# Turned rows with q lo twice for each head: score and state products on 128 rows instead of 64 and a padded state

## Chip, cores and metric

The kernel runs on one core of one Trainium2 chip. The metric is the device time of one execution in microseconds (us); the median of three runs stands for a kernel. Times inside an execution come from one profiled execution.

## What is computed

A gated linear attention over 768 tokens (4 sequences, 8 heads of 48), its rows through a gated product (the first MoE, dense, 1536 wide), and the result through eight experts, each token to the one with the largest logit.

```python
state = f[t][..., None] * state + k[t] outer v[t]     # f = sigmoid(f_logit), per batch and head, 48x48
y[t]  = q[t] @ state
x     = ((y @ w_a) * (y @ w_b)) @ w_out               # 3072 tokens x 384
e     = argmax(x @ w_gate)                            # of 8 experts
out   = gate * sigmoid(x @ w_output_gate)[e] * (relu(x @ w1[e]) @ w2[e])
```

All inputs are float32. The kernel keeps that precision by splitting every operand in a high and a low part (hi, lo) and adding the products that count.

## The kernel before

The 3072 tokens are 24 tiles of 128 (six chunks of each of four sequences); two tiles are one of 12 blocks. For each tile fourteen steps turn q, k, v and f into rows x of the attention; for each block the first MoE runs 12 times (`f` from 0 to 11) over `m_ab` (L816 to L818, 18 products) and `m_out` (L840 to L842, 6 products). Blocks 0 and 1 run while the weights are loaded and decoded: their order comes from a list of nominal times (T0, TAU). From block 2 on, `attend` (L1010) weaves the steps of the two tiles of the next block between the products of the present one, by the table `at`: for the first tile of a block scores at f = 4 and 5, for the second both at f = 6. The order on each engine is set at compile time by a scheduler that goes by program order, by readiness in its own timeline and by free buffers; some instructions are kept in program order by hand (`in_order`, L301). Tiles of one tag share its buffers.

The steps that matter here:

- `a_log` (L601) writes lh and ll, hi and lo of log f, one buffer each; `a_cum` (L633) sums them over the tokens with a triangular matrix (L636 for lh, L637 for ll) into a PSUM bank of tag "at", from which ScalarE makes eq and ek.
- `a_z` (L655) writes q and k, scaled, as float16 into z. Of a pair of heads it holds ten blocks of 64 columns: q hi twice for head 0, q hi twice for head 1, q lo for both heads, then k hi and lo, k lo and hi. On VectorE: L660 (k hi), L664 (q hi, twice), L665 (q lo); on GpSimd from tile 4 on: L661 (k lo). SyncE then issues one transposing DMA (L667) into zT, 20 blocks of 128 rows (four pairs of five). There is one zT buffer.
- `a_u` (L671) splits the state U before the chunk: hi on ScalarE (L683), lo on GpSimd (L684), and a copy of hi into U3, zero-padded to both heads, on GpSimd (L685).
- `a_kv` (L687) sums k times v of the chunk (L698 to L700), and VectorE updates U.
- `a_score` (L716), called twice a tile for four heads each: for each head a product on 128 rows (L726: k hi and lo against q hi twice) and one on 64 rows (L727: k hi against q lo). VectorE masks the result (sm, L729), ScalarE rounds it to Sh (L731), VectorE subtracts for Sl (L732).
- `a_av` (L737, L742 to L744) multiplies Sh and Sl by v; `a_inter` (L746) multiplies q by the state: for each pair two products of 48 columns (L758) and one of 96 columns (L760) of q lo with U3.
- `a_turn` (L766) and `a_x` (L777) turn the rows and split them into xh (ScalarE, L796) and xl (VectorE, L797), the moving operands of `m_ab` for the next block.

In the first blocks `conv_o` (L524) turns each of 12 pieces of w_out through two PSUM banks of tag "at" (L535, L545), the same tag as cumulative sums and scores.

Of the kernel before, what the change touches and what calls it, by code (L numbers as in the profile page):

```python
# [9 lines left out]
F16 = mybir.dt.float16  # L10
# [12 lines left out]
def general_path(nc, tc, q, k, v, f_logit, w_a, w_b, w_out, w_gate, w_ogate, w1, w2, out, cons):  # L23
    """the whole computation again, for values that the fast path doesn't carry"""
# [11 lines left out]
    with ExitStack() as ctx:  # L36
# [9 lines left out]
        # ---- recurrence over the tokens, one by one  # L46
# [52 lines left out]
        # ---- first MoE and the routing, 128 tokens at a time  # L99
        with tc.tile_pool(name="g_m1", bufs=1) as sp:  # L100
# [4 lines left out]
            for nm, w, n, m in (("a", w_a, KD, FF), ("b", w_b, KD, FF), ("o", w_out, NF, DM)):  # L105
                wt[nm] = tl("g_w" + nm, [P, n, m])
                for kk in range(n):
                    for c in range(m // DM):
# [39 lines left out]
                        # below float32's range: zero  # L148
# [98 lines left out]
        # ---- the experts, 128 slots at a time  # L247
# [57 lines left out]
def kernel(  # L305
# [46 lines left out]
    # ---------------------------------------------------------------- pools  # L352
# [17 lines left out]
    # ------------------------------------------------------------ constants  # L370
    # n(t): number of steps of the static slope up to token t of a chunk
# [72 lines left out]
    # routing state: (token, scale) per token, counts, sums of the softmax, ranges  # L444
# [9 lines left out]
    # DRAM scratch: rows of the first MoE by token (and a row of zeros), slot table  # L454
# [6 lines left out]
    # ---------------------------------------------------- weights, hi and lo  # L461
# [16 lines left out]
    def decoded(raw, n, on_pool):  # L478
        """384 columns of a weight as float32, times 2^WS"""
# [7 lines left out]
        # The upper word as a float has the double's exponent over 8. Times 2^(WS - 126) its  # L487
        # three upper exponent bits are clear, as long as the double is below 2^(128 - WS):
        # the sums tell. Below 2^(-112 - WS) it comes to nothing.
# [34 lines left out]
    def conv_o(f, raw, n, on_pool):  # L524
# [7 lines left out]
        # w_out @ [w_gate | w_output_gate] for these rows  # L532
# [18 lines left out]
    # -------------------------------------------------------------- attention  # L551
# [15 lines left out]
    # Heads in pairs, the first of a pair on the lower 64 partitions and the second on the upper:  # L567
    # of a pair, q hi twice for each head, q lo, k hi and lo, k lo and hi
    HP = H // 2
    z_n = [tl(f"z{n}", [P, HP, 10, 64], F16) for n in range(NZ)]  # L570
    U2 = [tl(f"U2{n}", [P, HP, 2, D], F16) for n in range(2)]
    U3 = [tl(f"U3{n}", [P, HP, 2, D], F16) for n in range(2)]
# [4 lines left out]
    for x in U2 + U3 + g_n:  # L577
        nc.gpsimd.memset(x, 0.0)

    def part(o):  # L580
        """the partitions of the pairs' first or second heads"""
        return slice(64 * o, 64 * o + D)
# [18 lines left out]
    def a_log(i):  # L601
        s = st[i]
        f, vin = s["f"], s["v"]
        nc.scalar.activation(out=f, in_=f, func=AF.Exp, scale=-1.0)
        nc.scalar.activation(out=f, in_=f, func=AF.Ln, scale=c_st, bias=c_st)
        s["lh"] = tl("lh", [P, H, D], F16)
        s["ll"] = tl("ll", [P, H, D], F16)
        nc.vector.tensor_copy(out=s["lh"], in_=f)
        fast(i).tensor_tensor(out=s["ll"], in0=f, in1=s["lh"], op=ALU.subtract)

    def squares(i, n, src, scale, junk):
        """the sum of squares of every token's row"""
# [42 lines left out]
    def a_z(i):  # L655
# [3 lines left out]
        kh, kl = z[:, :, 6:10:3, :D], z[:, :, 7:9, :D]  # L659
# [5 lines left out]
        nc.vector.tensor_tensor(out=z[:, :, 4:6, :D], in0=qe, in1=z[:, :, 0:4:2, :D], op=ALU.subtract)  # L665
        s["T"] = tl("zT", [P, 5 * HP, P], F16, 1)
# [4 lines left out]
    def a_u(i):  # L671
        """the state before this chunk, hi and lo"""
# [6 lines left out]
        if c > 0:  # L679
            u2, u3 = s["u2"], s["u3"] = U2[i % 2], U3[i % 2]  # L680
            for o in range(2):
                hi, lo = u2[part(o), :, o], u2[part(1 - o), :, o]
                nc.scalar.activation(out=hi, in_=U[b][part(o)], func=AF.Copy)  # L683
                nc.gpsimd.tensor_tensor(out=lo, in0=U[b][part(o)], in1=hi, op=ALU.subtract)  # L684
                nc.gpsimd.tensor_copy(out=u3[part(o), :, o], in_=hi)  # L685

    def a_kv(i):  # L687
# [6 lines left out]
        for h in range(H):  # L694
            a, o = divmod(h, 2)
            kh, kl = s["z"][:, a, 6 + 3 * o], s["z"][:, a, 7 + o]
# [19 lines left out]
    def a_score(i, u):  # L716
# [6 lines left out]
        for j in range(4):  # L723
            half = slice(64 * u, 64 * u + 64)
            k2, ql = T[:, 5 * j + 3 + u], T[half, 5 * j + 2]
            nc.tensor.matmul(sc[:, j], k2, T[:, 5 * j + u], start=True, stop=False)  # L726
            nc.tensor.matmul(sc[:, j], k2[half], ql, start=False, stop=True)  # L727
# [18 lines left out]
    def a_inter(i):  # L746
# [8 lines left out]
        for a in range(HP):  # L755
            for o in range(2):
                first_of = a == 0 and o == 0
                nc.tensor.matmul(pi[:, 2 * a + o], T[:, 5 * a + o], s["u2"][:, a, o], start=first_of, stop=False)  # L758
            two = pi[:, 2 * a : 2 * a + 2]
            nc.tensor.matmul(two, T[:, 5 * a + 2], s["u3"][:, a], start=False, stop=(a == HP - 1))  # L760
# [5 lines left out]
    def a_turn(i):  # L766
        """rows to columns by DMA, two bytes at a time: the words' lower and upper halves apart"""
# [37 lines left out]
    # -------------------------------------------------------------- first MoE  # L805
# [81 lines left out]
    def r_rank(j):  # L887
        """every token's slot: its expert's base and the tokens before it"""
# [19 lines left out]
    def free_order(key, ins):  # L908
        """scatters of one table go to rows of their own: they don't wait for each other"""
# [50 lines left out]
    # ------------------------------------------------------- experts' weights  # L960
# [3 lines left out]
    def load_expert(e, g, part):  # L964
        """two f-tiles of the e-th expert in line: part 0 of w1, part 1 of w2"""
# [23 lines left out]
    # --------------------------------------------------- program, first phase  # L989
# [10 lines left out]
    def route(j, f):  # L1000
        """the tokens of block j, sent to their experts in steps"""
# [50 lines left out]
    # the first two blocks run while the weights come: emission by nominal time  # L1052
# [41 lines left out]
    # -------------------------------------------------------------- second MoE  # L1094
    # The experts stand in a line: first the one with the most tokens before the last block, then
    # the others by their number of tokens, most first, each place with slots of its own number.
    # No token of the last block goes to the first half of the first place's slots, so these can
    # start before that block ends.
# [14 lines left out]
    def tiles_of(e):  # L1113
        """tiles of the e-th place: first slot and size"""
# [12 lines left out]
    def choose_first():  # L1127
        """the expert with the most tokens before the last block gets the first place"""
# [24 lines left out]
    def first_tokens(n):  # L1153
        """half n of the first place's slots"""
# [17 lines left out]
    def e_turn(e, u):  # L1172
        """rows to columns by DMA, two bytes at a time: the words' lower and upper halves apart"""
# [50 lines left out]
    def e_h(e, f, n=None):  # L1224
        """the first product of the e-th place for f, or of half n of the first place"""
# [4 lines left out]
        # hi, then lo with the tokens of a pair first: both parts of these stand together  # L1230
# [17 lines left out]
    def is_pair(m):  # L1248
        """a tile so small that both parts of h stand beside each other in one product"""
# [56 lines left out]
    def line_up(pc):  # L1306
        """the experts in their line, and whether one has too many tokens for its place"""
# [46 lines left out]
    def check_path():  # L1354
        """anything that the fast path doesn't carry: values out of its range or overfull experts"""
# [36 lines left out]
    def ahead(e, turn, columns, f):  # L1392
        """the input of the e-th place, while the one before is computed"""
# [144 lines left out]
```

## Time and profile before

| | |
|---|---|
| median of 3 runs | 931.11 us (930.51 to 933.27) |
| span of the profiled execution | 931.4 us |
| TensorE busy | 862.8 us, 93% |
| TensorE weight loads busy | 797.7 us, 86% |
| VectorE busy | 549.6 us, 59% |
| ScalarE busy | 448.0 us, 48% |
| GpSimd busy | 360.0 us, 39% |

The profiled execution has its span as its own time; it lies 0.3 us above the median. An instruction's duration on TensorE runs from its start to its modelled end, and products overlap: what a product costs in a dense series is seen from start to start, not from its duration. "Idle before" is the time that the engine stood before a group, with what ended it. The last part of the span, from some 627 us on, has no attention in it: it is the last block and the experts.

### The profile page before, as it was taken

What the parts mean: (1) busy time and instruction counts of PE and PEld (TensorE: products, weight loads), DVE (VectorE), ACT (ScalarE), POOL (GpSimd) and SP (SyncE); (2) the same over time, 40 slices, a digit from 0 to 9 for tenths busy, and PEclk for the clock granted to TensorE, in tenths of its full rate; (3) what the DMA queues carried; (4) which work ended last, traced back from release to release, by engine and by line L of the source; (5) the groups of instructions that cost most, each with busy time, mean ns of one, the idle gap of its engine ahead of it and who ended that gap; (6) DMA issues with size and microseconds to landing.
All of it is one profiled execution on the core that took longest, in us unless ns stands there. A gap on an engine that the chain in (4) does not pass through costs nothing.

```text
span 931.4 us, 18145 instructions
## 1 busy us (share of the span) xinstructions
PE 862.8 (93%) x6733; PEld 797.7 (86%) x6733; DVE 549.6 (59%) x1289; ACT 448.0 (48%) x1104; POOL 360.0 (39%) x428
## 2 busy tenths in 40 slices
PE   2689789989999999999999999999978999999993
PEld 1477789978989898989899999999878999999993
DVE  8887875554746474646555565642546666666630
ACT  6756655533545454536454554432424434445530
POOL 4444664352535353535445363412344231131111
PEclk9997999989999999999999999999989999999997
DMA  9874535462516252443526161211348644665610
GB/s 202 186 167 137 158 89 111 88 69 55 107 38 122 38 116 44 90 71 57 95 43 117 36 124 20 60 33 50 122 120 225 172 125 159 189 175 155 185 58 22
DMA packets 247756, 98.53 MB, mean 106 GB/s; under 512 B 210600, under 2 KB 243717, under 8 KB 247658
## 3 DMA queue, kind: packets, MB, share of 16 engines
q1 hardware_dynamic: 242538, 87.22, 42.3%
q0 software_dynamic: 4320, 10.03, 3.5%
q8 instruction: 55, 0.90, 0.4%
q14 instruction: 43, 0.35, 0.1%
q10 hardware_dynamic: 800, 0.02, 0.1%
HBM read 63.56 MB, written 10.49 MB: 80 GB/s over the span
## 4 chain that ended last, share of the span: by engine, by line
PE 70%; DMA 9%; DVE 8%; issue 7%; ACT 2%; POOL 2%; SPq 0%; POOLq 0%; DVEq 0%; ACTq 0%
PE ps_ab L816 9%; PE ps_ab L817 9%; PE ps_ab L818 9%; PE ps_out L301 5%; PE ps_out L842 4%; PE ps_out L841 4%; PE ps_yk L301 4%; PE ps_out L840 4%; PE ps_ab L1221 3%; PE ps_ab L1220 3%; PE ps_ab L1222 3%; PE ps_at L727 3%; PE ps_at L726 3%; DMA slots<-info,di 2%; DMA zT<-z 2%
## 5 line engine op out<-in xcount | busy, mean ns | idle before, releaser
L816 PE MATMUL ps_ab<-xh,wab 128*128 128x256 f32 x864 | 253.0, 293 | 5.5 <-DVE gf L824 3.8
L817 PE MATMUL ps_ab<-xl,wab 128*128 128x256 f32 x864 | 248.8, 288 | 0.5 <-DVE xl L797 0.5
L818 PE MATMUL ps_ab<-xh,wab 128*128 128x256 f32 x864 | 248.5, 288 | 0.2 <-POOL wab L520 0.2
L828 POOL TENSOR_TENSOR gl<-gf,gh 128x256 fp32r<-128x256 f32 x144 | 111.6, 777 | 244.7 <-ACT gh L827 243.3
L816 PEld LDWEIGHTS ps_ab<-xh,wab 128*128 128x128 f32 x864 | 167.1, 194 | 9.4 <-DVE gf L824 4.7
L817 PEld LDWEIGHTS ps_ab<-xl,wab 128*128 128x128 f32 x864 | 167.1, 193 | 2.3 <-DVE xl L797 1.8
L818 PEld LDWEIGHTS ps_ab<-xh,wab 128*128 128x128 f32 x864 | 167.2, 193 | 0.7 <-POOL wab L520 0.3
L824 DVE SCALAR_TENSOR_TENSOR gf<-ps_ab,asb 128x256 f32<-128x256 f32 x144 | 60.3, 419 | 81.4 <-ACT asb L823 76.0
L827 ACT ACTIVATE gh<-gf 128x256 fp32r<-128x256 f32 x144 | 59.9, 417 | 93.4 <-DVE gf L824 90.0
L841 PE MATMUL ps_out<-wo,gh 128*128 128x400 f32 x264 | 93.0, 352 | 2.2 <-DVE wo L547 2.2
L842 PE MATMUL ps_out<-wo,gl 128*128 128x400 f32 x264 | 92.2, 357 | 2.2 <-POOL gl L828 2.2
L840 PE MATMUL ps_out<-wo,gh 128*128 128x400 f32 x264 | 89.9, 348 | 1.3 <-ACT wo L546 1.3
L1294 POOL DMA_INDIRECT out_dram<-ys,tab x29 | 30.0, 1033 | 145.4 <-ACT ys L1289 139.9
L823 ACT ACTIVATE asb<-ps_ab 128x256 f32<-128x256 f32 x144 | 54.4, 379 | 58.1 <-PE ps_ab L818 57.9
L1221 PE MATMUL ps_ab<-xsl,wab 128*128 128x256 f32 (+5 forms) x216 | 73.5, 341 | 0.1
L1220 PE MATMUL ps_ab<-xsh,wab 128*128 128x256 f32 (+5 forms) x216 | 73.5, 341 | 0.1
L1222 PE MATMUL ps_ab<-xsh,wab 128*128 128x256 f32 (+5 forms) x216 | 73.3, 339 | 0.0
L977 DVE TENSOR_TENSOR wab<-raw,wab 128x768 fp32r<-128x768 f32 x48 | 46.6, 972 | 40.4 <-ACT wab L301 40.0
L1234 ACT ACTIVATE h<-ps_ab 128x256 fp32r<-128x256 f32 (+5 forms) x72 | 34.7, 483 | 69.3 <-PE ps_ab L1222 64.6
L1238 DVE SCALAR_TENSOR_TENSOR h<-ps_ab,h 128x64 fp32r<-128x64 f32 (+5 forms) x96 | 41.1, 450 | 36.7 <-ACT h L1234 36.7
L729 DVE TENSOR_TENSOR sm<-ps_at,mask 128x512 f32<-128x512 f32 x48 | 33.0, 688 | 45.0 <-PE ps_at L727 44.8
L732 DVE TENSOR_TENSOR Sl<-sm,Sh 128x512 f16<-128x512 f32 x48 | 33.9, 706 | 40.0 <-ACT Sh L731 40.0
(261 smaller groups left out, 1977.7 us busy)
## 6 DMA issues: line engine op xcount, KB each, us to landing
raw<-in_moe_w_dram SPq DMA_DIRECT2D x64, 384.0 KB
in_f<-in_f_logit_dram SPq DMA_DIRECT2D x24, 192.0 KB
in_q<-in_q_dram SPq DMA_DIRECT2D x24, 192.0 KB
in_k<-in_k_dram SPq DMA_DIRECT2D x24, 192.0 KB
in_v<-in_v_dram SPq DMA_DIRECT2D x24, 192.0 KB
raw<-in_moe_w_a_dram SPq DMA_DIRECT2D x12, 384.0 KB
raw<-in_moe_w_b_dram SPq DMA_DIRECT2D x12, 384.0 KB
raw<-in_moe_w_out_dram SPq DMA_DIRECT2D x12, 384.0 KB
```

The lines of the kernel that those rows point to most:

```text
L301: return lambda *a, **k: tc.keep_in_program_order(op(*a, **k))
L816: nc.tensor.matmul(pab[:, a], wh[:, kk, o : o + P], xh[:, kk], start=(kk == 0), stop=False)
L817: nc.tensor.matmul(pab[:, a], wh[:, kk, o : o + P], xl[:, kk], start=False, stop=False)
L818: nc.tensor.matmul(pab[:, a], wl[:, kk, o : o + P], xh[:, kk], start=False, stop=(kk == KD - 1))
L824: nc.vector.scalar_tensor_tensor(out=gf, in0=pab[:, 1], scalar=2.0**-WS, in1=asb, op0=ALU.mult, op1=ALU.mult)
L828: nc.gpsimd.tensor_tensor(out=gl, in0=gf, in1=gh.bitcast(F32), op=ALU.subtract)
L840: nc.tensor.matmul(o, gh[:, ts], wh[:, u], start=(f == 0), stop=False)
L841: nc.tensor.matmul(o, gh[:, ts], wl[:, u], start=False, stop=False)
L842: nc.tensor.matmul(o, gl[:, ts], wh[:, u], start=False, stop=(f == NF - 1))
L1220: nc.tensor.matmul(ph, wh[:, kk, o : o + P], sh[:, kk, us], start=(kk == 0), stop=False)
L1221: nc.tensor.matmul(ph, wh[:, kk, o : o + P], sl[:, kk, us], start=False, stop=False)
L1222: nc.tensor.matmul(ph, wl[:, kk, o : o + P], sh[:, kk, us], start=False, stop=(kk == KD - 1))
```

## The change

z has twelve blocks for each pair instead of ten: q hi twice for each head, then q lo twice for each head, then k hi and lo of the first head, k hi and lo of the second. One more copy on VectorE for each tile writes q lo a second time. zT has 24 blocks of 128 rows instead of 20. The second score product of a head takes the same 128-row operand as the first, against q lo twice, so that k lo times q lo is added, which was left out. The state products are two of 48 columns for each head, both on 128 rows with the same u2; U3 and its two copies for each tile go. To make room, lh and ll take the buffers of Sh and Sl (tags "Sh" and "Sl", one buffer each). Comments were removed in other places, so later lines keep their text and shift a little.

```diff
+    NB = 6
     HP = H // 2
-    z_n = [tl(f"z{n}", [P, HP, 10, 64], F16) for n in range(NZ)]
+    z_n = [tl(f"z{n}", [P, HP, 2 * NB, 64], F16) for n in range(NZ)]
-    U3 = [tl(f"U3{n}", [P, HP, 2, D], F16) for n in range(2)]
...
-        s["lh"] = tl("lh", [P, H, D], F16)
-        s["ll"] = tl("ll", [P, H, D], F16)
+        s["lh"] = ab.tile([P, H, D], F16, name="lh", tag="Sh")
+        s["ll"] = ab.tile([P, H, D], F16, name="ll", tag="Sl")
...
-        kh, kl = z[:, :, 6:10:3, :D], z[:, :, 7:9, :D]
+        kh, kl = z[:, :, 8:12:2, :D], z[:, :, 9:12:2, :D]
...
-        nc.vector.tensor_tensor(out=z[:, :, 4:6, :D], in0=qe, in1=z[:, :, 0:4:2, :D], op=ALU.subtract)
-        s["T"] = tl("zT", [P, 5 * HP, P], F16, 1)
+        ql = z[:, :, 4:8:2, :D]
+        nc.vector.tensor_tensor(out=ql, in0=qe, in1=z[:, :, 0:4:2, :D], op=ALU.subtract)
+        nc.vector.tensor_copy(out=z[:, :, 5:8:2, :D], in_=ql)
+        s["T"] = tl("zT", [P, NB * HP, P], F16, 1)
...
-            u2, u3 = s["u2"], s["u3"] = U2[i % 2], U3[i % 2]
+            u2 = s["u2"] = U2[i % 2]
...
-                nc.gpsimd.tensor_copy(out=u3[part(o), :, o], in_=hi)
...
-            kh, kl = s["z"][:, a, 6 + 3 * o], s["z"][:, a, 7 + o]
+            kh, kl = s["z"][:, a, 8 + 2 * o], s["z"][:, a, 9 + 2 * o]
...
-            half = slice(64 * u, 64 * u + 64)
-            k2, ql = T[:, 5 * j + 3 + u], T[half, 5 * j + 2]
-            nc.tensor.matmul(sc[:, j], k2, T[:, 5 * j + u], start=True, stop=False)
-            nc.tensor.matmul(sc[:, j], k2[half], ql, start=False, stop=True)
+            k2 = T[:, NB * j + 4 + u]
+            nc.tensor.matmul(sc[:, j], k2, T[:, NB * j + u], start=True, stop=False)
+            nc.tensor.matmul(sc[:, j], k2, T[:, NB * j + 2 + u], start=False, stop=True)
...
-                first_of = a == 0 and o == 0
-                nc.tensor.matmul(pi[:, 2 * a + o], T[:, 5 * a + o], s["u2"][:, a, o], start=first_of, stop=False)
-            two = pi[:, 2 * a : 2 * a + 2]
-            nc.tensor.matmul(two, T[:, 5 * a + 2], s["u3"][:, a], start=False, stop=(a == HP - 1))
+                u2 = s["u2"][:, a, o]
+                nc.tensor.matmul(pi[:, 2 * a + o], T[:, NB * a + o], u2, start=True, stop=False)
+                nc.tensor.matmul(pi[:, 2 * a + o], T[:, NB * a + 2 + o], u2, start=False, stop=True)
```

## Rows read from the trace of the kernel before

**Rows 1.** The page, busy time of each engine over the span.

```profile
PE 862.8 (93%) x6733; PEld 797.7 (86%) x6733; DVE 549.6 (59%) x1289; ACT 448.0 (48%) x1104; POOL 360.0 (39%) x428
```

**Rows 2.** Busy time by stage: PE, PEld, DVE, ACT, POOL, clock, DMA share, GB/s.

```profile
0.00:140.00 140.00, 100.77 (x746) 83.25 (x747) 117.73 (x247) 88.71 (x246) 71.89 (x88) 0.94 0.65 156
140.00:200.00 60.00, 60.00 (x558) 55.62 (x557) 35.97 (x98) 30.62 (x88) 27.46 (x36) 1.00 0.54 94
...
215.00:627.00 412.00, 411.19 (x3678) 379.00 (x3678) 231.83 (x579) 200.79 (x530) 178.38 (x223) 1.00 0.38 70
```

**Rows 3.** Timeline of TensorE, one score step: start, duration, line, rows*columns, shapes.

```profile
350.84 0.23 PE L726 MATMUL ps_at<-zT 128*128 128x128 f16 x1
351.00 0.23 PE L727 MATMUL ps_at<-zT 64*128 64x128 f16 x1
...
352.12 0.39 PE L816 MATMUL ps_ab<-xh,wab 128*128 128x256 f32 x1
```

**Rows 4.** Timeline of TensorE, dense series on 128 rows, and what follows.

```profile
362.68 0.18 PE L742 MATMUL ps_yk<-vv,Sh 128*128 128x48 f16 x1
...
363.11 0.18 PE L744 MATMUL ps_yk<-vv,Sl 128*128 128x48 f16 x1
363.13 0.22 PE L726 MATMUL ps_at<-zT 128*128 128x128 f16 x1
...
375.01 0.34 PE L636 MATMUL ps_at<-lh,tri 128*128 128x384 f16 x1
375.18 0.19 PE L744 MATMUL ps_yk<-vv,Sl 128*128 128x48 f16 x1
...
375.38 0.18 PE L743 MATMUL ps_yk<-vv,Sh 128*128 128x48 f16 x1
```

**Rows 5.** Groups of TensorE's weight loads by line: count | busy us, mean ns | idle before.

```profile
L726 PEld LDWEIGHTS <-zT 128*128 128x128 f16 x192 | 18.7, 98 | 20.8 <-DMA zT<-z 7.0 <-issue 2.3
```

**Rows 6.** Busy time by stage of line L726 alone: PE, PEld (counts in brackets).

```profile
0.00:140.00 140.00, 8.78 (x32) 3.42 (x32) 0.94 0.65 156
...
215.00:627.00 412.00, 31.02 (x136) 12.91 (x135) 1.00 0.38 70
```

**Rows 7.** Timeline of ScalarE around 203 us: idle before, and what ended it.

```profile
203.32 0.52 ACT L604 ACTIVATE in_f<-in_f 128x384 f32<-128x384 f32 x1 [8.27 <-DMA in_f<-in_f_logit_dram]
```

**Rows 8.** Timeline of TensorE, state products of one tile.

```profile
221.26 0.20 PE L760 MATMUL ps_yk<-U,zT 128*128 128x96 f16 x1
...
221.54 0.20 PE L760 MATMUL ps_yk<-U,zT 128*128 128x96 f16 x1
```

**Rows 9.** Timeline of SyncE's queue, transposes of a block's first and second tile.

```profile
339.59 2.93 SPq L667 DMA_TRANSPOSE zT<-z  x1
...
357.67 3.07 SPq L667 DMA_TRANSPOSE zT<-z  x1
```

**Rows 10.** The chain that ended last, around 407 us: start, length, what.

```profile
406.97 6.04 DMA zT<-z
```

**Rows 11.** Timeline of VectorE, lh for the next pair of tiles.

```profile
337.70 0.35 DVE L608 CAST lh<-in_f 128x384 f16<-128x384 f32 x1
```

**Rows 12.** Timeline of GpSimd, k lo of a block's first tile.

```profile
338.39 1.17 POOL L661 TENSOR_TENSOR z<-ek,z 128x384 f16<-128x384 f32 x1 [1.10 <-DVE z L660]
```

**Rows 13.** Timelines of GpSimd and TensorE: tile 4's ll, and its cumulative product.

```profile
48.90 2.51 POOL L609 TENSOR_TENSOR ll<-in_f,lh 128x384 f16<-128x384 f32 x1 [3.58 <-DVE lh L608]
...
134.21 0.29 PE L545 MATMUL ps_at<-wg,woT 128*128 128x16 f32 x2
134.35 0.32 PE L636 MATMUL ps_at<-lh,tri 128*128 128x384 f16 x1
```

**Rows 14.** Timelines of VectorE and TensorE where a block begins.

```profile
332.16 0.56 DVE L797 TENSOR_TENSOR xl<-xt,xh 128x384 fp32r<-128x384 f32 x1 [0.59 <-ACT xh L796]
333.66 0.34 PE L637 MATMUL ps_at<-ll,tri 128*128 128x384 f16 x1
...
334.36 0.28 PE L816 MATMUL ps_ab<-xh,wab 128*128 128x256 f32 x1
```

More of the change, by code (lines that the diff above doesn't have):

```diff
@@ L576 @@
         nc.gpsimd.memset(x[:, :, :, D:], 0.0)
-    for x in U2 + U3 + g_n:
+    for x in U2 + g_n:
         nc.gpsimd.memset(x, 0.0)
@@ L679, in a_u @@
         if c > 0:
-            u2, u3 = s["u2"], s["u3"] = U2[i % 2], U3[i % 2]
+            u2 = s["u2"] = U2[i % 2]
             for o in range(2):
                 hi, lo = u2[part(o), :, o], u2[part(1 - o), :, o]
-                nc.scalar.activation(out=hi, in_=U[b][part(o)], func=AF.Copy)
-                nc.gpsimd.tensor_tensor(out=lo, in0=U[b][part(o)], in1=hi, op=ALU.subtract)
-                nc.gpsimd.tensor_copy(out=u3[part(o), :, o], in_=hi)
+                own = U[b][part(o)]
+                nc.scalar.activation(out=hi, in_=own, func=AF.Copy)
+                nc.gpsimd.tensor_tensor(out=lo, in0=own, in1=hi, op=ALU.subtract)
     def a_kv(i):
```

## The prediction

> **What bounds the kernel now.** I read the page's busy shares first, then the busy time by stage, then the timeline of TensorE inside one attention step. The page says TensorE is busy for 93% of the span [rows 1]; a share is an average, so the stages decide. In the first 140 us TensorE is busy for 100.8 of 140 us while VectorE is for 117.7: there the weights are decoded, and TensorE's time is not the bound. From 140 to 200 us and from 215 to 627 us it is busy without a break (60.0 of 60, 411.2 of 412), at the full clock, while VectorE, ScalarE and GpSimd stay between 43% and 60% [rows 2]. In these stages a nanosecond of TensorE is a nanosecond of the span. There the attention of two later tiles is woven between the first MoE's products of each block of 256 tokens.
>
> Busy time hides the waste inside, so look at the starts. One score step (four heads) is eight products of 128 columns, alternately on 128 rows (L726) and on 64 (L727). From its first start to the start of what follows it takes 350.84 to 352.12 us, 1.28 us, so 160 ns a product [rows 3]. Neighbours on 128 rows are far denser: from 362.68 to 363.11 us lie 17 steps between products of 48 columns, 25 ns each, every one with a weight load of its own; and L636 of 384 columns (375.01) is followed after 170 ns [rows 4]. Between these two, 128 columns of float16 should come every 25 + 80/336 x 145 = 60 ns. So 100 ns of the 160 is no streaming. It has the size of one unhidden weight load: the load of L726 takes 98 ns [rows 5], and 98 + 60 = 158. Two consecutive products in the dense series have the same kind of load and the same kind of accumulation into one PSUM region; only the change of row count is peculiar to the score step. I conclude that a load for another row count is not run ahead under the product before it.
>
> The Trainium skill says in "TensorEngine Tiling (Array Packing)", Key Properties, that changing the tiling mode drains TensorE; the 160 ns agree. The same section says that different tiles can run loads and products in parallel, which would make the 64-row form the cheap one; these rows don't show that, as every product waits its full turn. What it would give stands under the third rival.
>
> **The change, part by part.** *Score products.* Each step keeps eight products of 128 columns and eight loads, all on 128 rows: k hi+lo against q hi, then against q lo. A step should take 8 x 60 = 0.48 us for 1.28, a gain of 0.80 us. L726 comes four times a step, and 136 times between 215 and 627 us [rows 6]: 34 steps, all in the saturated stage, 34 x 0.80 = 27.3 us. Bounds of the spacing: 25 ns (48 columns) and 170 ns (384 columns); the interpolation holds since both ends are float16 on 128 rows.
>
> The Trainium skill's "TensorE: Matmul & The Clock Gate", Back-to-back issue gap, gives about 81 ns for sustained load-and-product pairs of 128 columns. By that figure a step gains 0.64 us, the 34 steps 21.6 us, and the time would be an estimated 911 us; no row here has that very shape.
>
> Of the 48 steps of 24 tiles eight lie ahead of 140 us (32 times L726) [rows 6], so six between 140 and 215. That stretch is saturated at first, but ends in a stall: ScalarE, in order, waits 8.27 us until 203.32 us for a load of f [rows 7], and TensorE runs dry behind it. Part of what TensorE gains before is waited away there. Six steps are 4.8 us; between 0 and 4.8 I take half, 2.4. For the eight ahead of 140 us, where VectorE and the decode of weights set the pace, I take 0, and 3 us to either side, since buffers and the PSUM banks tie these tiles to the weights.
>
> *State products.* Twelve a tile become sixteen, all of 48 columns. Now three products (two of 48, one of 96 columns) take 0.093 us (221.26 to 221.54 for three such sets) [rows 8], so 0.37 us for a tile; sixteen at 25 ns are 0.40. Twenty tiles: 0.5 us more. The two GpSimd copies of the padded state go; GpSimd is 43% busy in that stage [rows 2], so I count them at nothing.
>
> *The transpose.* 24 blocks for 20. The issue holds SyncE for 3.07 us [rows 9]; at the same rate 3.7, so 0.6 us more of DMA. First tile of a block: issued at 339.59, used at 350.84 us [rows 3, 9]; at the 6.04 us of the slow case below that leaves 5 us to spare. Second tile: it starts when the state products of the first have read zT, at 357.67, and its first score product starts at 363.13 us [rows 4, 9], 5.46 us later. TensorE has other products there, but the margin is used up: the chain of waits shows the same transpose one block (49.3 us) on, 6.04 us from issue to use [rows 10]. So between 0 and 1.1 us (0.6 longer, with up to 0.5 already missing) for nine tiles: 0 to 10 us. I take 0.3 us each, 2.7 us, the row at 357.67 being the nearer to a usual one (its issue takes 3.07 us and TensorE doesn't wait).
>
> *The q lo copy.* One more float16 copy of 128x384 on VectorE for each tile. Nearest row: the cast of that shape, 0.35 us [rows 11]. For the first tile of a block the transpose is issued at 339.59 us, right behind GpSimd's subtraction of k lo, which ends at 339.56 [rows 9, 12], so that is the later one; the second tile's waits until the only zT buffer is free. So the copy is hidden in the saturated stage; without that cover it is 0.4 us a tile against the 5 us that the first tile has to spare. In the decode stage it is 6 x 0.35 = 2.1 us of VectorE, inside the 3 us above.
>
> *lh and ll move into the buffers of Sh and Sl.* This adds waits on a buffer. Today lh for the next pair is written a block ahead (337.70 us) and first read by L636 at 375.01 us [rows 4, 11], while the Sh of two tiles come and go. With one buffer for both, someone waits. If buffers go out in program order, lh waits for the last products that read Sh and Sl, shortly behind 375.38 us [rows 4]. Then come the cast of 0.35 us, the subtraction, for which the k lo one of 1.17 us is the nearest row [rows 12], and the cumulative product, possible by about 377.5. The second half of that product runs today at 333.66 us [rows 14], in the block after at 383, so it can keep its place. Queued behind it are ScalarE's exponentials and the transpose of the first tile, with 5 us to spare; behind lh on VectorE stand the copies that turn the second tile, 0.35 us. I cost this at nothing. That buffers go out in program order is seen at the PSUM banks of one tag: the subtraction for tile 4 starts on GpSimd at 48.90 us, but its cumulative product runs at 134.35 us, in the gaps of the last-but-one piece of w_out, exactly its place in the written order, though TensorE had idle time in between [rows 2, 13].
>
> *Last thing of a block.* The next block's products need xl of the second tile, ready at 332.72; the first product starts at 334.36 us [rows 14], 1.6 us of slack. All four steps lie ahead of that chain, so it moves up with them, less the transpose's 0.6.
>
> **The sum**, against the profiled execution (span 931.4 us; the three runs have a median of 931.11, so nothing has to be added around it): 27.3 + 2.4 - 0.5 - 2.7 = 26.5 us less, 904.9 us. I forecast 905.
>
> **Rivals.**
> *The added transfer is paid in full.* Nine second tiles lose 1.1 us each, the decode stage loses 3, the six steps give nothing: 27.3 - 0.5 - 9.9 - 3 = 13.9, so 917 us. For it: the 6.04 us; against: TensorE has other products ready at that point.
> *Slower: the shared buffer goes to the next pair's lh first.* If it went to whoever is ready, lh at 337.70 would hold it until 375.01, and Sh of the tile scored from 350.84 on would wait for some 20 us in each of nine blocks. The block's own products hide perhaps half, the rest is idle: 9 x 10 to 9 x 20 us, less the 27, so about 1000 to 1090 us, 1050 in the middle. It decides as soon as more than 3 us of it is unhidden in a block. Against it: the program order in [rows 13].
> *The row count is not what costs 160 ns.* Then nothing is gained, and the transposes and state products cost 3 us: 934 us, unless hidden: 931 to 934. Against it: the 25 and 170 ns on 128 rows [rows 4]. Here belongs the rule of the Trainium skill on parallel tiles, named above.
>
> **How the numbers follow.** Forecast 0.75, paid transfer 0.15, slower 0.06, no gain 0.04. The range takes in the bounds of the forecast (all six steps and 3 us of the decode stage gained: 931.4 - 27.3 - 4.8 - 3 = 896) and the first rival: 895 to 919, which leaves out the other two and a part of the spacing's bound. About 0.3% (2.8 us) is what a measurement can tell from no change: faster 0.91, same 0.03, slower 0.06.
>
> **What would show it.** Right: score products at about 60 ns from start to start, a step at half a us, the block of 49.3 us at 46 to 47; no new wait at the first products of a block. The transpose: issue 3.7 us, waits for zT of some tenths at second tiles. Wrong: a spacing of 80 ns or more; TensorE waiting for Sh or for the cumulative product's inputs; a block that still takes 49 us with TensorE idle inside; or a decode stage that ends after 145 us.

## The result, and the profile after

The changed kernel takes 911.4 us (909.1 to 913.2); the kernel before took 932.2 us beside it. The ratio is 0.977, with a 95% interval of 0.975 to 0.980. The forecast was 905 us, the range 895 to 919: the sign and the range are right, and 6 us of the 26 are missing. The profiled execution after has a span of 910.0 us. All times here are of a kernel's fast runs; one run of the second kernel below (952.2 us, at a lower granted clock than its others) was a slow one and is left out.

The page's busy shares of the changed kernel, which answer to [rows 1]:

```profile
PE 824.6 (91%) x6813; PEld 785.2 (86%) x6813; DVE 551.9 (61%) x1313; ACT 445.3 (49%) x1104; POOL 333.9 (37%) x386
```

Its windows by stage (us, then busy time of PE, PEld, DVE, ACT, POOL, clock, DMA share, GB/s), which answer to [rows 2]:

```profile
0.00:140.00 140.00, 96.73 (x787) 86.99 (x787) 121.00 (x254) 89.93 (x249) 73.04 (x85) 0.93 0.69 162
140.00:200.00 60.00, 55.65 (x545) 52.65 (x538) 35.07 (x100) 29.01 (x82) 23.64 (x28) 1.00 0.70 104
215.00:608.00 393.00, 384.65 (x3729) 369.08 (x3729) 231.19 (x592) 198.68 (x533) 157.40 (x194) 0.99 0.44 79
```

TensorE lost 38.2 us of busy time, but the span lost only 21.4. The saturated stage is no longer saturated: TensorE is idle for 8.4 us of 393, where before it was for 0.8 of 412. The timeline of TensorE in one score step (start, duration, line, rows*columns) and, ahead of the next step, its wait; it answers to [rows 3]:

```profile
343.11 0.23 PE L727 MATMUL ps_at<-zT 128*128 128x128 f16 x1
343.18 0.22 PE L728 MATMUL ps_at<-zT 128*128 128x128 f16 x1
343.24 0.22 PE L727 MATMUL ps_at<-zT 128*128 128x128 f16 x1
343.29 0.22 PE L728 MATMUL ps_at<-zT 128*128 128x128 f16 x1
...
343.54 0.36 PE L816 MATMUL ps_ab<-xh,wab 128*128 128x256 f32 x1
...
355.19 0.23 PE L727 MATMUL ps_at<-zT 128*128 128x128 f16 x1 [1.10 <-DMA zT<-z]
```

Score products now start every 56 ns (median of the trace; 107 ns where the granted clock is 0.5), and the step shown takes 0.43 us instead of 1.28. But at the second tile of a block TensorE stands still for 1.10 us until zT is there. SyncE's queue for the same block, which answers to [rows 9]:

```profile
332.52 3.54 SPq L669 DMA_TRANSPOSE zT<-z  x1
348.47 3.83 SPq L669 DMA_TRANSPOSE zT<-z  x1
```

And the row of TensorE's waits (line, waited for: us in total, times, longest):

```profile
PE ps_at L727 <- DMA zT<-z: 21.7, 11, 5.1
```

The row of before reads 6.1 us, 4 times. Tile by tile, the second tiles of the nine blocks from 200 us on wait 11.3 us (3.94 in block 2, then 0.0 to 2.0), before 1.3 us. A block, 49.3 us before, takes 46.3 to 47.3 us (blocks 3 to 8), and block 2, with the longest wait, 57.0 instead of 55.0. What made zT late was the question for the runs.

### The profile page after: what moved, and what is told of

It is laid out like the page before. It is cut to its first block, busy times and chain, and to the rows that moved or that the text cites. A ratio compares the mean times of both kernels' runs of the same rounds, so it can differ in the third digit from the quotient of the medians.

```text
span 910.0 us, 18331 instructions
## 1 busy us (share of the span) xinstructions
PE 824.6 (91%) x6813; PEld 785.2 (86%) x6813; DVE 551.9 (61%) x1313; ACT 445.3 (49%) x1104; POOL 333.9 (37%) x386
## 4 chain that ended last, share of the span: by engine, by line
PE 37%; DMA 22%; DVE 15%; issue 10%; ACT 7%; POOL 4%; SPq 3%; POOLq 0%; DVEq 0%; ACTq 0%
DMA zT<-z 6%; PE ps_ab L817 4%; PE ps_ab L816 4%; PE ps_ab L818 4%; DMA in_f<-in_f_logit_dram 4%; PE ps_out L301 4%; DMA slots<-info,di 3%; PE ps_yk L301 3%; DMA raw<-in_moe_w_dram 3%; DMA turned<-halves 2%; PE ps_ab L1220 2%; PE ps_ab L1221 2%; PE ps_ab L1222 2%; PE ps_out L842 2%; PE ps_out L841 2%
## 5 line engine op out<-in xcount | busy, mean ns | idle before, releaser
L828 POOL TENSOR_TENSOR gl<-gf,gh 128x256 fp32r<-128x256 f32 x144 | 115.2, 800 | 223.1 <-ACT gh L827 212.8
L841 PE MATMUL ps_out<-wo,gh 128*128 128x400 f32 x264 | 93.1, 353 | 1.8 <-DVE wo L547 1.8
L840 PE MATMUL ps_out<-wo,gh 128*128 128x400 f32 x264 | 91.8, 354 | 0.0
L301 ACT ACTIVATE wab<-raw 128x768 fp32r<-128x768 f32 x48 | 40.4, 841 | 35.3 <-DMA raw<-in_moe_w_dram 35.0
```

Of the source, the lines that this page charges most:

```text
L301: return lambda *a, **k: tc.keep_in_program_order(op(*a, **k))
L828: nc.gpsimd.tensor_tensor(out=gl, in0=gf, in1=gh.bitcast(F32), op=ALU.subtract)
L840: nc.tensor.matmul(o, gh[:, ts], wh[:, u], start=(f == 0), stop=False)
L841: nc.tensor.matmul(o, gh[:, ts], wl[:, u], start=False, stop=False)
```

## The experiments

The kernels are numbered, first to twelfth, in the order in which they were made. Each was timed beside the kernel before, whose median then lay between 930.6 and 935.7 us; the ratios are to that. A kernel's own runs spread over 2 to 13 us, so differences of 2 us are not told from nothing. Each trace is of one execution.

**Rows alone.** The kernel before, with the second score product on 128 rows against the block that holds q lo of both heads; z, zT and lh, ll as before. It adds k lo times q lo of the other head, of the size that is left out before.

```diff
-            k2, ql = T[:, 5 * j + 3 + u], T[half, 5 * j + 2]
+            k2, ql = T[:, 5 * j + 3 + u], T[:, 5 * j + 2]
-            nc.tensor.matmul(sc[:, j], k2[half], ql, start=False, stop=True)
+            nc.tensor.matmul(sc[:, j], k2, ql, start=False, stop=True)
```

> The kernel before with one change: the second score product takes all 128 rows of k hi and lo against the block that holds q lo of both heads, so it adds k lo times the other head's q lo, a term of the size of those left out. Ten blocks, U3, lh and ll as before. If the row count alone is worth 0.83 us a step and the rest of the change costs the missing 5 to 10 us (longer transposes, shared buffer): 931.5 less 28 to 31, so 900 to 904, score products at 56 ns, blocks of 46.0 to 46.4 us, waits for zT in the blocks at most 2 us in all. If instead the blocks are held by chains of latency, whatever shortens the scores: 908 to 912, blocks of 46.9 us, with waits at the second tile's scores as in the changed kernel.

899.7 us (897.7 to 903.3), ratio 0.967 [0.964, 0.969]: 31 us less. Without any of the other edits the row count gives more than the whole change does. Blocks 3 to 8 take 46.0 to 47.3 us. The waits for zT at second tiles are 5.6 us, not at most 2 as expected; 4.4 of them stand in block 2.

**Rows undone.** The changed kernel with the second product on 64 rows again.

```diff
-            nc.tensor.matmul(sc[:, j], k2, T[:, NB * j + 2 + u], start=False, stop=True)
+            half = slice(64 * u, 64 * u + 64)
+            nc.tensor.matmul(sc[:, j], k2[half], T[half, NB * j + 2 + u], start=False, stop=True)
```

> The changed kernel with the second score product back on 64 rows (k hi against one copy of q lo); twelve blocks, shared buffers and state products stay. If the row count is the gain: products alternate at 160 ns again, 34 steps in the saturated stage lose 28 us, less the waits for zT that the longer steps cover: 934 to 940, at or above the kernel before. If the row count is not the gain: 910 to 914.

939.8 us (936.3 to 944.4), ratio 1.009 [1.006, 1.012]: 28 us more than the changed kernel, and some 9 us more than before. (The second head of a pair multiplies k lo, not k hi, with q lo here.) The timeline of TensorE, same columns:

```profile
352.32 0.23 PE L727 MATMUL ps_at<-zT 128*128 128x128 f16 x1
352.48 0.23 PE L729 MATMUL ps_at<-zT 64*128 64x128 f16 x1
352.64 0.23 PE L727 MATMUL ps_at<-zT 128*128 128x128 f16 x1
```

160 ns again. The two runs agree on the row count: 31 us from one side, 28 from the other.

**Shared buffers alone.** The kernel before with lh and ll in the buffers of Sh and Sl.

```diff
-        s["lh"] = tl("lh", [P, H, D], F16)
-        s["ll"] = tl("ll", [P, H, D], F16)
+        s["lh"] = ab.tile([P, H, D], F16, name="lh", tag="Sh")
+        s["ll"] = ab.tile([P, H, D], F16, name="ll", tag="Sl")
```

> The kernel before with lh and ll in the buffers of Sh and Sl, nothing else. If the sharing costs nothing: 929 to 934. If the sharing is what ate the missing gain: 936 to 942, with TensorE waiting for Sh, Sl or lh. If it goes to the next pair's lh first: 1000 and more.

938.9 us (934.5 to 940.2), ratio 1.007 [1.005, 1.010]: the edit that I had costed at nothing costs some 7 us, within the second theory's range; but the longest wait that it adds is for zT, not for Sh, Sl or lh. Block 2 begins 3.1 us later than before and block 4 7.1 us later; the blocks after it are as long as before (49.0 to 49.6 us). Timelines of VectorE (lh of tile 4) and of TensorE (first score product of tile 6):

```profile
88.39 1.16 DVE L608 CAST lh<-in_f 128x384 f16<-128x384 f32 x1
...
204.65 0.29 PE L726 MATMUL ps_at<-zT 128*128 128x128 f16 x1 [5.30 <-DMA zT<-z]
```

lh of tile 4 waits for its buffer until 88.39 us; before it was cast at 48.40 us. So buffers go out in program order, as forecast; the price of that stands in the first four blocks, which the forecast had looked at only for products.

**Rows, and no padded state.** The first kernel, in which the product of q lo with the state takes u2 of both heads instead of U3; U3 and its copies go. It adds q lo of one head times U lo of the other, again of the size left out.

```diff
-                nc.gpsimd.tensor_copy(out=u3[part(o), :, o], in_=hi)
-            nc.tensor.matmul(two, T[:, 5 * a + 2], s["u3"][:, a], start=False, stop=(a == HP - 1))
+            nc.tensor.matmul(two, T[:, 5 * a + 2], s["u2"][:, a], start=False, stop=(a == HP - 1))
```

> As e1_rows_alone, and the state products of q lo take u2 of both heads (96 columns, all 128 rows) in the place of the padded copy U3, whose two GpSimd copies a tile go; ten blocks, own buffers for lh and ll. GpSimd is not the bound: within 3 us of e1_rows_alone, so 898 to 904. If GpSimd's copies do hold something: 5 us or more below e1_rows_alone.

897.5 us (896.3 to 898.2), ratio 0.964 [0.962, 0.966]: the fastest of all, 14 us ahead of the changed kernel, with ten blocks a pair and buffers of their own for lh and ll. At second tiles TensorE waits 0.3 us in all: block 2's 4.4 us of the first kernel is gone, and block 3 begins 4.3 us sooner than there.

**The same with shared buffers, and with the longer transpose.** The fifth kernel is the fourth with the diff of the shared buffers; the sixth also has twelve blocks a pair, two of them unused.

> The kernel of the fourth experiment (rows of both products 128, ten blocks a pair, no padded state; 897.5 us), and in it lh and ll in the buffers of Sh and Sl, as the change has them. Theory C (the sharing costs about 7 us whatever the score products take, since it acts in the decode stage and in blocks 2 and 3): 903 to 907 us, block 2 starts some 3 us later, blocks 4 to 8 stay at 46.0 to 46.5. Rival (with shorter score steps TensorE has less to hide the late lh behind, so the sharing costs in every block): 909 to 913 us, blocks 4 to 8 at 46.8 or more, and nothing of the distance to the changed kernel (911.4) would be left for the transpose. Second rival (the sharing only cost where the decode stage was as it was; here it is free): 896 to 900 us.

> The fifth kernel with the transpose of the change alone: twelve blocks a pair instead of ten, of which two hold zeros and are read by nobody; no second copy of q lo, twelve state products a tile. Against the fifth kernel this is the price of the four added blocks; against the changed kernel (911.4 us) it lacks the copy and four state products a tile. Theory D (the longer transpose is what is left of the distance): 3 to 7 us over the fifth kernel, 907 to 912 us, waits for zT at second tiles of 9 us or more in all, blocks 9 and 10 some 2 to 4 us longer than in the fifth. Rival (the added copy and state products are what is left): within 1.5 us of the fifth kernel, 903 to 907 us, waits for zT as there.

909.6 us (907.2 to 912.0), ratio 0.976 [0.973, 0.979], and 909.9 us (906.8 to 913.1), ratio 0.977 [0.973, 0.980]. Theories C and D fell, and what their rivals say came, but for single blocks (block 7 of the fifth kernel takes 45.7 us). Sharing costs 12 us here, more than on the kernel before, and it costs in the steady blocks too: second tiles wait 7.4 us for zT, in blocks 3 to 6 2.46, 1.11, 1.35 and 0.71 us. The four added blocks cost 0.4 us, nothing that can be told, with second tiles waiting 6.4 us. So by the times nearly the whole distance from the fourth kernel to the changed one is the sharing, and 7.4 of its 12 us stand at zT. That the blocks are free holds beside shared buffers only: no kernel has twelve blocks and buffers of their own for lh and ll.

**The transpose in two parts.** The first part has two buffers, so that it needn't wait for the tile before: ten blocks of twenty in the fifth kernel (shared buffers), five in the fourth (own buffers).

```diff
-        s["T"] = tl("zT", [P, 5 * HP, P], F16, 1)
-        nc.sync.dma_start_transpose(out=s["T"], in_=z.rearrange("p a c d -> p (a c d)"))
+        TA = tl("zA", [P, 10, P], F16, 2)
+        nc.sync.dma_start_transpose(out=TA, in_=z[:, :2].rearrange("p a c d -> p (a c d)"))
+        TB = tl("zB", [P, 5 * HP - 10, P], F16, 1)
+        nc.sync.dma_start_transpose(out=TB, in_=z[:, 2:].rearrange("p a c d -> p (a c d)"))
```

> The fifth kernel (lh and ll in the buffers of Sh and Sl, 909.6 us) with the transpose of each tile cut in two halves of ten blocks, the first with two buffers, so that half of a second tile is turned before the first tile lets go. Theory E (what sharing costs beyond the decode stage is TensorE waiting for the second tile's zT: 7.4 us at second tiles from 200 us on, because the transpose is there issued and landed with no margin): these waits fall to about 1 us, 901 to 904 us, blocks 3 to 8 at 46.0 to 46.5. Rival (the waits for zT only stand where another late step would otherwise be met: the late lh and ll set the pace of the block): the waits turn up at other lines, 908 to 911 us.

> The fourth kernel (lh and ll in their own buffers, no padded state, 897.5 us) with the transpose cut in a part of one pair with two buffers and a part of three pairs with one; more does not fit beside. Theory E: TensorE waits there only 0.3 us at second tiles, so little can be gained: 896 to 898 us. Rival (two transposes for one hold SyncE and the DMA engines longer, which the first tile of a block or the loads behind it pay): 899 to 903 us.

910.2 us, ratio 0.973 [0.969, 0.978], and 903.5 us, ratio 0.968 [0.964, 0.972]. In the first the waits at second tiles are gone and blocks 3 to 8 take 46.0 to 47.0 us but for one of 49.8; yet block 2 begins at 180.4 us instead of 174.2, and the gain is lost there. Its rival's time came, not its reason. The kernel before ran at 935.7 us beside these two, 3 us slower than beside the fifth, so by the ratios the first is 2 us faster than the fifth and the second 4 us slower than the fourth. I haven't traced what the second transpose holds up in the decode stage; the other kernel, too, begins block 2 later (175.3 for 173.5 us). Inconclusive on the cause; as a remedy it is worth little or nothing.

**What stands ahead of the transpose.** In the fifth kernel TensorE reaches the second tile's scores no sooner than in the fourth: in block 5 the score products come 5.59 us behind the issue in the fourth kernel without a wait, and would come 5.74 us behind it in the fifth. It is the transfer that is late. The windows of that stretch, from the issue on (us, PE, PEld, DVE, ACT, POOL, clock, DMA share, GB/s), first the fourth kernel, then the fifth:

```profile
340.20:343.60 3.40, 3.40 (x42) 3.37 (x41) 0.69 (x1) 1.80 (x4) 0.55 (x1) 1.00 0.73 137
343.60:345.10 1.50, 1.50 (x15) 1.45 (x14) 0.42 (x1) 0.55 (x2) 0.56 (x1) 1.00 0.68 126
```

```profile
347.60:351.00 3.40, 3.40 (x42) 3.37 (x39) 0.81 (x2) 2.17 (x5) 1.21 (x2) 1.00 0.73 138
351.00:352.50 1.50, 1.50 (x15) 1.45 (x14) 0.30 (x1) 0.42 (x1) 0.00 (x0) 1.00 2.59 65
```

For 3.4 us they are alike; then the fifth moves half the bytes at four times the DMA share: packets hang. By the packets of the trace the last of this transpose lands 4.39 us after its issue in the fourth kernel and 6.53 in the fifth. What the two have different ahead of it stands in GpSimd's queue, rows of the fourth kernel first, then of the fifth (with a row of ScalarE and of VectorE):

```profile
333.43 0.99 POOL L942 DMA_INDIRECT slots<-info,di  x1 [0.58 <-DVE di L931]
334.73 0.97 POOL L942 DMA_INDIRECT slots<-info,di  x1 [0.31 <-issue]
...
340.21 3.04 SPq L666 DMA_TRANSPOSE zT<-z  x1
```

```profile
340.02 0.17 DVE L931 CAST di<-df 128x2 uint32<-128x2 f32 x1
...
341.26 0.53 ACT L603 ACTIVATE in_f<-in_f 128x384 f32<-128x384 f32 x1 [3.44 <-DMA in_f<-in_f_logit_dram]
...
342.17 0.73 POOL L825 TENSOR_TENSOR gl<-gf,gh 128x256 fp32r<-128x256 f32 x1 [3.49 <-ACT gh L824]
343.05 0.99 POOL L942 DMA_INDIRECT slots<-info,di  x1 [0.15 <-issue]
344.35 0.98 POOL L942 DMA_INDIRECT slots<-info,di  x1 [0.30 <-issue]
...
347.61 3.04 SPq L666 DMA_TRANSPOSE zT<-z  x1
```

The two scatters of a block's routing (each token's number and weight to a table in memory) are sent by GpSimd. In the fourth kernel they go as soon as their addresses di are there, 5.5 us ahead of the transpose. With shared buffers the compiled order puts a subtraction (gl) in front of them, which waits for ScalarE, which waits for a load of f; di is there at 340.02, but the scatters go at 343.05 and 344.35, 3.3 us ahead of the transpose. Before the change it was 7.1 us, in the changed kernel 5.2. So I moved the scatters: the steps that rank a block's tokens and send them run at f = 2 instead of 3 (the fifth kernel, the changed kernel and, as a control, the fourth), or at f = 4 (the fourth).

```diff
-        if f == 3:
+        if f == 2:
             r_rank(j)
             r_send(j)
```

> The fifth kernel (shared buffers, 909.6 us) with the ranks of the block's tokens and the two scatters to slots one product group earlier (f = 2 instead of 3). In the fifth kernel the scatters go out 2 to 4 us before the second tile's transpose, in the fourth 5 to 7 us. Theory F (sharing pushes GpSimd's scatters up to the transpose, and the transpose lands late behind them): the landing of second tiles returns to 4.4 to 5.2 us after the issue, waits for zT at second tiles fall from 7.6 to under 2.5 us, 901 to 905 us. Rival (it is instruction loads on the same DMA engines, or the late lh and ll themselves): waits as before, 908 to 911 us.

> The fourth kernel (own buffers, 897.5 us) with the same two scatters one product group later (f = 4), so that they go out just ahead of the second tile's transpose. Theory F: waits for zT at second tiles rise from 0.3 us to 4 us or more, 901 to 906 us. Rival (scatters do not matter): 896 to 899 us.

> The fourth kernel (own buffers, 897.5 us) with the scatters one product group earlier (f = 2), the control for the ninth. Theory F: TensorE waits there for zT at second tiles only 0.3 us in all, so there is nothing to win: 895 to 899 us, unless the scatters now meet the loads of the next tiles, as in the eleventh kernel, which would cost: 899 to 905 us. Rival (an earlier scatter is worth 9 us of its own, whatever the buffers, so the ninth kernel says nothing on sharing): 887 to 890 us.

Measured, with the landing counted from the trace's packets; "ahead" is from the second scatter's issue to the transpose's, both as medians over the second tiles of blocks 3 to 10, the waits those at second tiles of blocks 2 to 10:

| kernel | scatter ahead | transpose lands after | waits for zT | time |
|---|---|---|---|---|
| before | 7.0 us | 4.4 us (to 5.6) | 1.3 us | 931 us |
| 4th: own buffers | 5.5 | 4.7 (to 5.5) | 0.3 | 897.5 |
| 5th: shared | 3.0 | 5.8 (to 7.7) | 7.4 | 909.6 |
| 9th: shared, scatters early | 7.6 | 4.4 (to 5.1) | 2.8 | 900.8 |
| 10th: own, scatters late | 2.1 | 5.9 (to 8.6) | 19.0 | 929.3 |
| 12th: own, scatters early | 6.6 | 4.7 (to 5.6) | 0.7 | 899.2 |
| changed (24 blocks) | 5.1 | 5.7 (to 6.3) | 11.3 | 911.4 |

Ratios: 0.964 [0.960, 0.968] for the ninth, 0.995 [0.992, 0.998] for the tenth, 0.965 [0.961, 0.968] for the twelfth. The earlier scatter gives the fifth kernel 9 us back and the fourth nothing, so it isn't worth something of its own; sent late, it costs the fourth kernel 32 us. The ranking steps moved with the scatters; the runs don't part the two.

Single transfers say more than medians. The eight kernels with 20 blocks in one transpose (before, first, third, fourth, fifth, ninth, tenth and twelfth) have 64 second-tile transposes in blocks 3 to 10. In 37 of them no load of instructions longer than 0.5 us was under way. Of these, 13 were sent 6.6 to 7.6 us behind the second scatter, and all landed 4.4 us after their issue; 15 were sent 4.3 to 6.0 us behind, and twelve landed at 4.4 us, three at 4.6 to 5.1; nine were sent 1.8 to 3.7 us behind, and two landed at 4.4 us, seven at 5.0 to 8.6. Nearness alone doesn't decide it: in block 9 of the fifth kernel the transpose, 2.8 us behind, lands at 4.4 us.

For the changed kernel itself the scatters explain less. Seven of its eight second-tile transposes in blocks 3 to 10 have a load of instructions of 0.8 to 2.1 us under way, and these seven land late, 5.35 to 6.31 us after their issue. The eighth, 4.9 us behind the scatter, has none and lands at 5.0 us, which is as early as any of 24 blocks. In the DMA queues of the changed kernel from 348 to 355 us, the transpose shown above, the load is this row (packets, MB, share):

```profile
q8 instruction: 1, 0.02, 1.0%
```

Block 2's wait, 3.9 of the 11.3 us, stands before a transpose that lands at 5.0 us; there the issue was late for TensorE, not the landing. How much of the changed kernel's waits is owed to scatters, to loads of instructions and to the longer transfer, the runs don't part.

Back to the tenth kernel. Timelines of GpSimd, SyncE and TensorE in the tenth kernel:

```profile
351.60 0.97 POOL L942 DMA_INDIRECT slots<-info,di  x1 [0.30 <-issue]
353.40 3.08 SPq L666 DMA_TRANSPOSE zT<-z  x1
...
361.93 0.29 PE L723 MATMUL ps_at<-zT 128*128 128x128 f16 x1 [4.11 <-DMA zT<-z]
```

Its row of TensorE's waits:

```profile
PE ps_at L723 <- DMA zT<-z: 23.2, 8, 4.7
```

The 32 us are more than the waits for zT. Moving the ranks also makes score products wait 4.3 us, in three waits, for a PSUM bank that VectorE still reads (dj), and between 250 and 520 us some 20 us are granted half the clock, where the fourth kernel has the full one throughout.

> The changed kernel (911.4 us) with the scatters one product group earlier. Theory F: waits for zT at second tiles fall from 11.3 us to some 4 us (24 blocks land at 5.0 us at best, so there is less room than with 20), 903 to 907 us. Rival: 910 to 913 us.

920.6 us (915.6 to 924.9), ratio 0.987 [0.983, 0.990]: above what either theory expected. In the profiled execution, the fastest of the six, waits for zT did fall, from 11.3 to 5.7 us (4.3 of them in block 2), but blocks 4 and 9 take 50.8 and 50.0 us. Timelines of SyncE, GpSimd and ScalarE in block 4:

```profile
290.45 1.10 SPq L301 DMA_DIRECT2D in_f<-in_f_logit_dram  x1
...
290.55 1.05 POOL L945 DMA_INDIRECT slots<-info,di  x1 [0.30 <-DVE di L934]
291.90 0.98 POOL L945 DMA_INDIRECT slots<-info,di  x1 [0.30 <-issue]
...
297.19 0.53 ACT L604 ACTIVATE in_f<-in_f 128x384 f32<-128x384 f32 x1 [6.66 <-DMA in_f<-in_f_logit_dram]
```

Here the scatters meet the load of f, sent at 290.45: it lands at 297.2, 6.7 us later, in the changed kernel 3.9 us (292.34 to 296.23). ScalarE waits for it in order, and behind it stand the evictions of the gated product: the stall of [rows 7] again. The waits fell as the theory has it, though the loads of instructions under way changed with the move too; as a remedy the move depends on what else is in flight. This explains block 4; block 9 I haven't followed.

## Why the prediction was right in sign and range, and 6 us off

The times of the kernels split the change: 31 us less by the rows (before to the first), 2 less without the padded state (to the fourth), 12 more by sharing (to the fifth), 0.4 more by four blocks (to the sixth), 1.4 more by the copy and four state products (to the changed one). All but the first and the third are inside the spread. The traces, one execution each, split the time up to the start of block 11 otherwise: 30.1 less, 6.2 less, 10.0 more, 1.5 more, 5.7 more. The stage behind it, which no edit touched, takes 301 to 307 us from kernel to kernel and hides the difference. So the second and the last part may be larger than the times show; the first and the third stand either way. The price of sharing is that of the step from the fourth kernel to the fifth; the change with buffers of its own wasn't run.

- *What bounds the kernel, and the load for another row count.* Right, shown from both sides (the first and the second kernel). The spacing was forecast at 60 ns, measured 56; 34 x (1.28 - 0.43) = 28.9 us, forecast 27.3. The 81 ns that the Trainium skill gives in "TensorE: Matmul & The Clock Gate", Back-to-back issue gap, is not what this series shows; the same section's formula for an isolated product, 128 / 2.4 + 2.5 = 56, fits it. That the 911 us worked out from 81 ns is the measured time is chance.
- *Six early steps and the decode stage.* Forecast 2.4 with 3 to either side. With the rows alone block 3 begins 5.1 us earlier, in the changed kernel 2.4. The sharing can account for that: block 3 begins 2.3 us later in the fifth kernel than in the fourth.
- *State products and the padded state.* Forecast 0.5 more; going without U3 measured 2 us less, sixteen products and the copy 1.4 more. By the times neither can be told from nothing; up to block 11 they are 6.2 less and 5.7 more. The copy of q lo takes 0.25 us 13 times and some 0.64 or more 11 times, 0.44 in the mean, not 0.35.
- *The transpose.* Forecast 2.7 us, bounds 0 to 10, for four added blocks; they cost 0.4 us in the step from the fifth kernel to the sixth, where second tiles waited 7.4 us already. Right was that the margin of the second tile is used up, and that lost time would show there. But I read [rows 10], 6.04 us, as the size of the thing, and didn't ask what was in flight then. In the trace of before two loads of instructions by DMA (1.2 and 1.7 us) lie in just that transfer, none in the one of [rows 9].
- *lh and ll at nothing.* This is the step that failed, by the times of the fourth and fifth kernel. The order of buffers was right; the rival that gave the buffer to lh first fell (lh of tile 4 was cast at 82.9 us instead of 48.4, after its predecessors had let go). "Its place is kept" was argued from TensorE and from the queues of ScalarE and VectorE, but GpSimd's queue wasn't read, nor the decode stage for buffers. It measured 12 us, of which 9 come back in the fifth kernel when the scatters are moved.
- *The paid transfer, 917 us.* Its waits came in full (10.0 us more than before for its 9.9), but not as it has them: 3.9 us in block 2, none in block 8, not 1.1 in each. At the earliest 24 blocks land 5.0 us after their issue, 20 at 4.4, which is its 0.6 us; how much of the waits this is, no run shows. The time lies between it and the forecast.
- *What would show it.* Blocks of 46 to 47 us: nearly (46.3 to 47.3). Waits of some tenths at second tiles: wrong, up to 3.9 us. Issue of 3.7 us: 3.5 to 4.8 from block 3 on.

## What to carry to other kernels

Count products of unlike row counts that alternate as if nothing were pipelined between them, and price their removal from a dense series of the same trace. An edit that is free on TensorE can still reorder another engine's queue: read every queue whose instructions send a transfer, and for each transfer without slack ask what was sent shortly before it and what else, loads of instructions too, is under way with it. Before spending memory on a wider layout, try the narrow one: here a product against the block as it already lay gave more than the change, and cost no buffer.

## What I had not expected of the hardware

Two small scatters go with a delay of the transpose that is sent shortly behind them: of the nine that were sent 1.8 to 3.7 us behind with no long load of instructions under way, seven landed 5.0 to 8.6 us after their issue instead of 4.4. The load of f took 6.7 us instead of 3.9 in the one block followed where the scatters went out right behind its issue. The trace shows packets that hang for up to 2.8 us in the fifth kernel and 3.8 us in the tenth while few bytes move, but not why. It isn't the scatters' own bytes: in block 5 of the fifth kernel their last packet ends at 346.09 us, and the transpose's first starts at 348.77. The second scatter is reported as landed only at 353.69 us, 9.35 us after its issue and 0.45 us before the transpose's last packet ends. The Trainium skill, in "DMA: Bandwidth & Descriptors", Latency and other measured facts, names contention on the port of the rings that GpSimd's transfers use as a best guess for two engines that are usually slow; the packets in this trace carry no engine's number, so no run here shows whether it is that. Loads of instructions go with a delay too: in the kernel before the three transposes of second tiles from block 3 on with one of 1.0 to 1.7 us in them land at 4.8 to 5.6 us, the five others at 4.4.

After a wait for zT the granted clock was often at 0.5 (1.2 GHz for 2.4). At second tiles the fifth, the tenth and the changed kernel have ten waits of 1.9 to 4.7 us from block 2 on; after seven of them the clock stood at 0.5 or fell to it within 0.7 us, after three (1.9, 2.0 and 2.2 us) it didn't. In the fifth kernel's block 3, after 2.46 us, the score products go within one step from 60 to 107 ns apart, so such a wait costs more than its own length.
